# A finer passage into an MLP, z statistics on ScalarE, and eleven GpSimd operations behind VectorE's

## The chip, the cores and the metric

The kernel runs on one core of one Trainium2 chip. The metric is device time in microseconds (us) of one execution, lower is better. A core has TensorE (PE in the profile; PEld is its weight load), VectorE (DVE), ScalarE (ACT), GpSimd (POOL) and SyncE (SP, which here issues DMAs). Each engine runs its own instructions in order and waits on semaphores for the others.

## The reference

One sequence of 2048 rows with 640 channels goes through an adaptive-norm block: a gated long-convolution (an SSM with a short convolution in front), then a gMLP mixer.

```python
mod = (silu(c) @ w_mod)                    # sa, ca, ga, sb, cb, gb, each of 640
h = layernorm(x) * (1 + ca) + sa
x = x + ga * A(h, k, v, ...)               # A: 4-tap shift of k, times v, FFT convolution over 2048, times q
h = layernorm(x) * (1 + cb) + sb
x = x + gb * B(h, ...)

def B(x):
    z = gelu(x @ w_in)                     # 640 -> 1728
    z1 = z[..., :864]
    z2 = layernorm(z[..., 864:])           # mean and variance over 864, per row
    g = w_sp @ z2 + b_sp                   # 2048 x 2048 over the rows
    return (z1 * g) @ w_out                # 864 -> 640
```

## The kernel before, in words

**Parts.** The first part (the convolution) works in five units of 128 channels. It computes the long convolution with matrix products: stage 1, a forward transform per frequency pair (`fwd`), a product with the kernel's transform on VectorE (`prod`, L495), sums `W` of its parts on GpSimd or VectorE (`csum`, L509), an inverse transform (`inv`), and a copy of its result into `Z` on ScalarE (`zc`, L616 calling L278). A last product with the table `Ebd` gives the rows of y.

**The passage.** For units 0 to 3 `Z` is turned by a DMA. For unit 4, the last, TensorE turns it (`zfl`, L831, `last_stage_pe`): four tiles of eight 128x128 flips, two in PSUM slots `pu` and two in `pz`, each copied out whole (`zk`, 1024 elements a partition, two on VectorE and two on ScalarE). Then 32 products of 16 columns (`yl`) for each of four groups of four row tiles; those of the first group come in four pieces of eight. VectorE multiplies with the gate (`yml`, L856), adds the residual (`res`, L808), and takes the statistics of the rows (`ln2`, L814; `ag2`, L943). GpSimd makes 1/sqrt(var + eps) in two operations (`rstd2`, L218 and L219), VectorE -mean*rstd (`nmr2`, L947), and one of three engines normalizes a row tile into `xn2` (`zx`: ScalarE L957, GpSimd L959, VectorE L961). For the first group, in two pieces of two row tiles, TensorE flips the normalized tiles (`hfl`, L972), and VectorE and ScalarE modulate them into `hT` (`hmod`, L985 and L983). The other three groups are turned by a DMA (`turn`) and modulated in place (`hmod2`, L1011 and L1009).

**The z groups.** Sixteen row tiles in four groups. A product of a row tile with half of one half of `w_in` is five matmuls of 432 columns (`zz`, called through the helper L275). There are 64 such products, into the four PSUM slots `pu` and `pz` (two each). ScalarE applies GELU out of PSUM (`gelu`, L1034). The z2 half goes to an `X1` tile, z1 into the memory of the tables `M2` and `G2`. For z2, VectorE takes the statistics of each 432-column piece (`stz`, L1040) and joins them (`agz`, L1044); GpSimd makes the rstd (`rstdz`), VectorE `nmrz` (L1049), and VectorE or ScalarE normalizes (`zn`, L1057, L1055).

**The mixer and the projection.** A two-level Winograd-like scheme over blocks of `w_sp` and z2: sums `S` (L1101) and `T` (L1111), seven products per pair of row tiles (`prodw`, L1126), their joins, DMA turns of u (`turnu`, L1173), the output products (`pp`, `pq`, L1348 and L1335) and the output DMAs.

**What sets the order.** Nothing is scheduled by the compiler. Each operation is recorded with the keys that it reads and writes, and a string `ORDER` of engine letter and operation number sets on which engine and in which place each is emitted (`Plan.run`). Waits follow from the tiles that an instruction touches. `FILLS` is a list of dummy products of `ident` with 512 columns (`fill`) that write a slot nobody reads.

Of the kernel before, what the change touches and what calls it, by code (L numbers as in the profile page):

```python
# [1462 lines left out]
```

## Time and profile before

| | us |
|---|---|
| median of the timed runs (3) | 306.06 (305.61 to 306.27) |
| the profiled execution: its span, first to last instruction | 303.8 |
| between that span and the median | 2.26 |
| TensorE busy in the span | 293.1 |
| VectorE busy | 260.4 |
| GpSimd busy | 186.8 |
| ScalarE busy | 164.0 |

The profiled execution's own time is known by its span. Timeline rows give the start of an instruction in us from the start of the span, its duration, the engine, the line in the kernel, what it writes and reads, and in brackets how long the engine had stood idle and who released it. PEclk is the share of the full clock that TensorE was granted.

### The profile page before, as it was taken

The page shows a single profiled execution, that of the slowest core. Times are in us where ns is not written, and L with a number is a line of the kernel's source. Part 1 is how long each engine was busy: PE and PEld are TensorE (multiplying, and loading weights), DVE is VectorE, ACT ScalarE, POOL GpSimd, SP SyncE. Part 2 cuts the span into 40 slices and gives each one's busy share as a digit, 9 for nine tenths or more (in the row PEclk, how much of TensorE's full clock was granted, in tenths as well). Part 3 has the DMA queues.
Part 4 walks back from the last instruction along what each step waited for, and adds up shares of the span by engine and source line. Part 5 has one row for each costly group of instructions (what it writes and reads, how often), then busy time and mean ns, then how long its engine had stood idle before and what let it go on. Part 6 is the DMA issues. An engine that isn't in the chain of part 4 may idle for free.

```text
span 303.8 us, 7152 instructions
## 1 busy us (share of the span) xinstructions
PE 293.1 (96%) x2827; PEld 207.0 (68%) x2827; DVE 260.4 (86%) x527; ACT 164.0 (54%) x299; POOL 186.8 (61%) x213
## 2 busy tenths in 40 slices
PE   6899999999999999799999999999999999999996
PEld 2788999999989988645555555555555555665664
DVE  8899999999989999989595988988678798886794
ACT  5989999998888865446665779500111102111110
POOL 5463788839769997577537342099531863476771
PEclk9999999999999999869999999999999999999999
DMA  7999869792397978005997900057654446452433
GB/s 143 270 242 271 194 177 282 134 223 39 77 186 163 287 122 276 2 2 105 157 234 154 197 0 4 0 117 150 132 133 90 102 112 141 102 84 73 91 83 121
DMA packets 117155, 41.57 MB, mean 137 GB/s; under 512 B 102557, under 2 KB 117122, under 8 KB 117122
## 3 DMA queue, kind: packets, MB, share of 16 engines
q1 hardware_dynamic: 116968, 41.08, 62.0%
q8 instruction: 22, 0.36, 0.5%
q14 instruction: 11, 0.09, 0.1%
q10 hardware_dynamic: 154, 0.05, 0.1%
HBM read 16.60 MB, written 2.63 MB: 63 GB/s over the span
## 4 chain that ended last, share of the span: by engine, by line
PE 80%; DVE 8%; SPq 5%; DMA 3%; issue 2%; POOL 1%; ACT 0%; DVEq 0%; POOLq 0%
PE ps L1126 23%; PE pu L275 19%; PE pz L275 17%; PE po L1335 5%; PE sm L275 5%; PE s L275 4%; SPq L570 3%; DVE Tf L495 3%; PE po L1348 3%; DMA ZT<-in_A_v_dram 3%; PE pz L1126 2%; PE pu L1126 1%; DVE Z L616 1%; SPq L585 1%; DVE ot L1394 1%
## 5 line engine op out<-in xcount | busy, mean ns | idle before, releaser
L275 PEld LDWEIGHTS <-Z 128*128 128x128 bf16 x320 | 32.0, 100 | 28.8 <-issue 3.0
L275 PE MATMUL pu<-X,M 128*128 128x128 bf16 (+1 forms) x480 | 45.6, 237 | 0.9 <-DVE Tf L495 0.7
L509 POOL TENSOR_TENSOR W<-Tf 128x256 bf16<-128x256 f32 x42 | 30.7, 745 | 15.0 <-DVE Tf L495 9.0
L275 PEld LDWEIGHTS <-M 128*128 128x128 bf16 x480 | 36.7, 98 | 4.2 <-issue 1.6
L1126 PEld LDWEIGHTS <-S 128*128 128x128 bf16 x256 | 25.0, 98 | 20.8
L275 PE MATMUL pu<-big,Z 128*128 128x432 bf16 x160 | 34.6, 360 | 0.0
L278 ACT CAST X<-s 128x1024 bf16<-128x1024 f32 x32 | 32.7, 1021 | 3.3 <-PE s L275 3.2
L275 PE MATMUL pz<-big,Z 128*128 128x432 bf16 x160 | 33.0, 349 | 0.0
L495 DVE TENSOR_TENSOR Tf<-pu,KH 128x1024 f32<-128x1024 f32 x25 | 30.3, 1215 | 1.2 <-ACT Z L278 0.5
L1132 ACT COPY m<-ps 128x432 f32<-128x432 f32 x7 | 3.6, 521 | 49.8 <-PE ps L1126 41.0
L1126 PEld LDWEIGHTS <-wT 128*128 128x128 bf16 x192 | 18.8, 98 | 15.3
L278 ACT CAST Z<-pz 128x512 bf16<-128x512 f32 x40 | 23.5, 596 | 4.9 <-PE pz L275 4.7
L275 PEld LDWEIGHTS <-G 128*128 128x128 bf16 x330 | 24.6, 98 | 1.8 <-issue 0.4
L278 ACT CAST KH<-pu 128x512 bf16<-128x512 f32 x40 | 23.1, 592 | 3.8 <-PE pu L275 3.4
L1126 PE MATMUL ps<-X,wT 128*128 128x432 bf16 x112 | 22.7, 346 | 0.0
L1126 PE MATMUL ps<-X,S 128*128 128x432 bf16 x112 | 22.6, 346 | 0.0
L1040 DVE BATCH_NORM_STATS2 stz<-X 128x6 f32<-128x432 bf16 x32 | 18.1, 588 | 5.0 <-ACT X L1034 4.9
L1126 PE MATMUL ps<-T,S 128*128 128x432 bf16 x112 | 22.2, 346 | 0.0
L275 PE MATMUL sm<-dg,big 128*128 128x128 bf16 x320 | 20.7, 219 | 1.1 <-DVE Z L616 1.0
L275 PEld LDWEIGHTS <-big 128*128 128x128 bf16 x320 | 18.9, 98 | 2.0 <-issue 1.6
L495 DVE TENSOR_TENSOR T<-pu,KH 128x1024 bf16<-128x1024 f32 x15 | 18.2, 1215 | 1.9 <-PE pu L275 1.8
L275 PEld LDWEIGHTS <-X 128*128 128x128 bf16 x288 | 17.8, 98 | 2.2 <-POOL X L433 0.7
(223 smaller groups left out, 666.7 us busy)
## 6 DMA issues: line engine op xcount, KB each, us to landing
wm<-in_w_mod_dram SPq DMA_DIRECT2D x6, 800.0 KB, 4.9
xt<-in_A_q_dram SPq DMA_DIRECT2D x4, 640.0 KB, 5.6
out_dram<-ot SPq DMA_DIRECT2D x15, 160.0 KB, 1.9
big<-in_B_w_in_dram SPq DMA_DIRECT2D x2, 1080.0 KB, 7.8
X<-in_A_ssm_k_dram SPq DMA_DIRECT2D x4, 512.0 KB, 6.2
ZT<-in_A_v_dram SPq DMA_DIRECT2D x1, 1024.0 KB, 7.6
big<-in_A_v_dram SPq DMA_DIRECT2D x1, 1024.0 KB, 7.8
w_o<-in_B_w_out_dram SPq DMA_DIRECT2D x6, 160.0 KB, 3.5
```

Source lines behind the costliest of these rows:

```text
L275: nc.tensor.matmul(o, lhsT=w, rhs=x, start=start, stop=stop)
L278: (e.copy if e is nc.scalar else e.tensor_copy)(dst, src)
L495: e.tensor_tensor(T_[:], (tl[pu] if src is None else tl[src])[:, :, :, None, :].to_broadcast(shape), tl[KH][:, :, None, :, :].to_broadcast ...
L509: e.tensor_tensor(tl[W][:, :, o, :], T_[:, :, 0, o, :], T_[:, :, 1, 1 - o, :], op=ALU.add if o else ALU.subtract)
L570: e.dma_start_transpose(k_of(u)[:, KPAD + h * m:KPAD + (h + 1) * m], A_k[0, h * m:(h + 1) * m, u * DU:(u + 1) * DU])
L585: e.dma_start(v_of(0, ns.start, NT // n) if u0 == 0 else tl[name][:], v_nat[:, ns, ds])
L616: e.tensor_tensor(dst, tl[ps][:].rearrange("p n (c g) -> p n c g", g=8), v_of(u, i * SCH, SCH).rearrange("p n (c g) -> p n c g", g=8), op= ...
L1040: op("D", "stz", lambda e, i=i, n=n, fc=fc: e.bn_stats(out=stz[:, n, fc, :], in_=tl[z2][:, i, fc * FC:(fc + 1) * FC]), r=[(z2, (i, fc))], ...
L1126: nc.tensor.matmul(ps[:, :FC], lhsT=lhs[:, s_, :], rhs=rhs(s_), start=(s_ == 0 and not more), stop=(s_ == HT - 1), skip_group_check=more)
L1132: e.copy(part[p, m][:], part[p, BANK[m]][:, :FC])
L1335: nc.tensor.matmul(ps[:, :HS], lhsT=w(k), rhs=x(k), start=start and k == 0, stop=stop and k == n - 1, skip_group_check=True)
L1348: e.matmul(po[t, i][:, :hi - lo], lhsT=uTs[t][:fsz[ft], ft, :], rhs=T["w_o"][:fsz[ft], ft, lo:hi], start=(ft == 0), stop=(ft == NFT - 1))
```

## The change

Up to the middle of the last unit of the convolution both programs are the same, instruction by instruction. From there on the list `ORDER` is new, and six edits stand behind it:

- The last copy into `Z` (`zc` of step 4 of unit 4) is cut in two.
- The flips of unit 4 and their copies come in halves of four (`zfl`, `zk`, 512 elements), and the first group's `yl` in eight pieces of four.
- For the first two row tiles (`quick`) VectorE adds eps to the variance right after its statistics, so GpSimd makes the rstd in one operation (`rstdq`); `nmr2` is left out, and both tiles are normalized on VectorE. `hfl` flips tile by tile.
- `FILLS` has six more dummy products, in pieces of one, and the list puts them elsewhere.
- For z groups 0 and 1 ScalarE makes the statistics: the GELU of z2 also writes the sum of its outputs (`accum_out`), a new `zsq` squares the row tile with a sum, into memory that z1 of the last row tile takes later, and four small VectorE operations per group (`momz`) turn the sums into mean and variance. `stz` and `agz` of these groups are gone.
- A letter H in the list marks a GpSimd operation that waits until the last VectorE operation ahead of it in the list, of the kinds in `PORT`, has ended. Eleven are marked: `res`, `zx`, `gbm`, two `hmod2`, two `lsm`, `vsum`, two `usum`, `ssum`.

In the rows below `st` and `mv` are the row statistics, `gh` the gated branch, `xt` the residual rows, `s` and `sm` the PSUM slots of the flips, `Z` also the slot of `xn2` and `hT`; X is the z2 tile, M and G hold z1, and stz is where the sums go. The number of an engine's semaphore stands behind its name in a wait.

TensorE at the flips of unit 4, before, each kind of row once:

```order
L831 LDWEIGHTS Z [waits Activation_49]
L831 MATMUL pu<-ident,Z 128x128
L275 LDWEIGHTS ZT
L275 MATMUL sm<-Ebd,ZT 128x64 [waits DVE_49]
L275 MATMUL sm<-Ebd,ZT 128x64
L831 LDWEIGHTS Z
L831 MATMUL pz<-ident,Z 128x128
L831 MATMUL pz<-ident,Z 128x128 [waits PE_49]
```

and now:

```order
L856 LDWEIGHTS Z [waits Activation_49]
L856 MATMUL pu<-ident,Z 128x128
L856 LDWEIGHTS Z
L856 MATMUL pu<-ident,Z 128x128 [waits Activation_49]
L856 MATMUL pz<-ident,Z 128x128
L856 MATMUL pz<-ident,Z 128x128 [waits PE_49]
L856 MATMUL pz<-ident,Z 128x128 [waits DVE_49]
L295 LDWEIGHTS X
L295 MATMUL sm<-Ebd,X 128x4x4 [waits PE_49]
```

The second half of a slot's flips now has a wait of its own on the engine that copies the first half; three of the four slots show one.

VectorE from the statistics of the first two row tiles to their modulation, before:

```order
L814 BN_STATS st_72<-xt 128x6 x2
L943 BN_AGGR mv_82<-st_72 128x2 x2
L856 TENSOR_TENSOR gh<-gh,sm 128x2x128
L808 TENSOR_TENSOR xt<-xt,gh 128x4x128
L808 TENSOR_TENSOR xt<-xt,gh 128x2x128
L947 SCALAR_TENSOR_TENSOR nmr_84<-mv_82,rstd_83 128x2
L814 BN_STATS st_72<-xt 128x6 x4
L943 BN_AGGR mv_82<-st_72 128x2
L856 TENSOR_TENSOR gh<-gh,pz 128x4x128
L985 TENSOR_SCALAR Z<-s_2939,cb_col,sb_col 128x256 x3
```

and now:

```order
L837 BN_STATS st_72<-xt 128x6 x2
L973 BN_AGGR mv_82<-st_72 128x2 x2
L975 TENSOR_SCALAR mv_82<-mv_82 128x2
L884 TENSOR_TENSOR gh<-gh,sm 128x2x128
L884 TENSOR_TENSOR gh<-gh,pz 128x4x128
L831 TENSOR_TENSOR xt<-xt,gh 128x2x128
L993 TENSOR_SCALAR Z<-xt,mv_82,rstd_83 128x640 x2
L837 BN_STATS st_72<-xt 128x6 x2
L1021 TENSOR_SCALAR Z<-s_2920,cb_col,sb_col 128x256 x3
```

`nmr` is gone from the first piece, a small operation on `mv` and two normalizations have come in, and two multiplications with `gh` stand ahead of them. GpSimd there, before and now:

```order
L753 TENSOR_TENSOR gh<-gh,gsa_bf 128x4x128 x2
L218 TENSOR_SCALAR rstd_83<-mv_82 128x2
L219 TENSOR_TENSOR rstd_83<-rstd_83,mhalf 128x2
L959 TENSOR_SCALAR Z<-xt,rstd_83,nmr_84 128x640
L808 TENSOR_TENSOR xt<-xt,gh 128x4x128 x2
L218 TENSOR_SCALAR rstd_83<-mv_82 128x2
L219 TENSOR_TENSOR rstd_83<-rstd_83,mhalf 128x2
```

```order
L831 TENSOR_TENSOR xt<-xt,gh 128x4x128 x3
L238 TENSOR_TENSOR rstd_83<-mv_82,mhalf 128x2
L831 TENSOR_TENSOR xt<-xt,gh 128x4x128
L776 TENSOR_TENSOR gh<-gh,gsa_bf 128x4x128
L236 TENSOR_SCALAR rstd_83<-mv_82 128x2
L238 TENSOR_TENSOR rstd_83<-rstd_83,mhalf 128x2
L991 TENSOR_SCALAR Z<-xt,rstd_83,nmr_84 128x640
```

Of the first rstd's two GpSimd operations one is left, and it normalizes a tile less there.

ScalarE from the first modulation on, before:

```order
L957 ACTIVATE Z<-xt,nmr_84,rstd_83 128x640
L983 ACTIVATE Z<-sm,sb_col,cb_col 128x256 x2
L1034 ACTIVATE X_2980<-pu 128x432
L957 ACTIVATE Z<-xt,nmr_84,rstd_83 128x640
L1034 ACTIVATE M_80<-pz 128x432 x2
L1034 ACTIVATE M_80<-pu 128x432
L983 ACTIVATE Z<-sm,sb_col,cb_col 128x256 x2
L1034 ACTIVATE M_80<-pu 128x432
L957 ACTIVATE Z<-xt,nmr_84,rstd_83 128x640
L1034 ACTIVATE X_2980<-pz 128x432
```

and now:

```order
L1019 ACTIVATE Z<-sm,sb_col,cb_col 128x256 x2
L1071 ACTIVATE X_2983,stz<-pz 128x432
L1071 ACTIVATE X_2983,stz<-pu 128x432
L989 ACTIVATE Z<-xt,nmr_84,rstd_83 128x640
L1071 ACTIVATE X_2983,stz<-pu 128x432
L1019 ACTIVATE Z<-sm,sb_col,cb_col 128x256
L1071 ACTIVATE M_80<-pu 128x432
L1071 ACTIVATE X_2983,stz<-pz 128x432
L1019 ACTIVATE Z<-sm,sb_col,cb_col 128x256
L1071 ACTIVATE M_80<-pz 128x432
L989 ACTIVATE Z<-xt,nmr_84,rstd_83 128x640
```

The rows with `stz` write sums beside their result, and rows of 128x864 that write G are the squares.

The diff, cut to its core (of the list a few lines):

```diff
-FILLS = (4, 2, 2, 2, )
+LAST = 4
+PORT = {"nmr1", "nmr2", "nmrz", "ln1f", "momz", "e2a", "ghm", "res", "csum", "ssum", "xn", "zx", "hmod2", "oa", "usum", "zn", "tsum", "c22b", "lsm", "ox",
+        "c22m", "turns", "vsum", "vsum5", "gbm", "msgn", "mneg", "gneg", "f1m", "e2m", "addD"}
+ACT_STATS = (0, 1)
+FILLS = ((4,), (2,), (2,), (2,), (1, 1, 1), (1, 1, 1))
...
+P737 P739 P731 D740 G677 P727 P741 D732 P743 P746 P748 D698 D699 A738 P745 P747 A728 P744 P742 D749 D750 D751 P1046
+P1047 P1048 D752 P757 D780 P1040 S589 D781 P590 D753 D758 D754 P771 G782 D783 D784 H702 D756 A591 P597 A598 D701 P785
...
-    def run(self, engines):
-        order = [(x[0], int(x[1:])) for x in ORDER.split()]
-        assert sorted(i for _, i in order) == list(range(len(self.ops)))
+    def run(self, engines, tc):
+        nc = tc.nc
+        held = None
+        order = [(x[0].replace("H", "G"), int(x[1:]), x[0] == "H") for x in ORDER.split()]
+        assert sorted(i for _, i, _ in order) == list(range(len(self.ops)))
         done = set()
-        for e, i in order:
+        for e, i, gated in order:
             o = self.ops[i]
             assert e in o["eng"] and done.issuperset(o["deps"]), (e, i)
             if self.late is not None and i >= self.late[0]:
                 self.late[1]()
                 self.late = None
+            made = []
+            if e in "DG":
+                nc.push_inst_callback(made.append)
             o["fn"](engines[e])
+            if e in "DG":
+                nc.pop_inst_callback()
+            if e == "D" and o["kind"] in PORT:
+                held = made[-1]
+            elif gated and held is not None:
+                tc.add_manual_dep(made[0], held.name, mybir.DependencyInfo(mybir.DependencyClass.Sync, mybir.DependencyReason.SCHED_ONLY), reason="port")
             done.add(i)
...
-    def rstd_from_var(dst, var_ap):
-        nc.gpsimd.tensor_scalar(dst, var_ap, EPS, 1.0, op0=ALU.add, op1=ALU.mult)
-        nc.gpsimd.tensor_tensor(dst, dst, mhalf[:, 0:dst.shape[1]], op=ALU.pow)
+    def rstd_from_var(dst, var_ap, eps=True):
+        if eps:
+            nc.gpsimd.tensor_scalar(dst, var_ap, EPS, 1.0, op0=ALU.add, op1=ALU.mult)
+            var_ap = dst
+        nc.gpsimd.tensor_tensor(dst, var_ap, mhalf[:, 0:dst.shape[1]], op=ALU.pow)
...
+            parts = KP if u == NU - 1 and st == LAST else 1
+            for h in range(parts):
+                k0, k1 = h * KP // parts, (h + 1) * KP // parts
+                op("AD", "zc", lambda e, k0=k0, k1=k1: copy(e, tl[Z][:, :, 2 * (KP * st + k0):2 * (KP * st + k1), :], tl[pz][:, k0:k1]
+                                                            .rearrange("p k r (q c) -> p q (k r) c", c=4)),
+                   r=[pz, (Z, "new")], w=[(Z, (st, h) if parts > 1 else st)], n=parts)
...
-            op("GD" if u < NU - 1 else "D", "res", lambda e: e.tensor_tensor(sl, sl, gl, op=ALU.add),
+            op("GD" if u < NU - 1 or g else "D", "res", lambda e: e.tensor_tensor(sl, sl, gl, op=ALU.add),
...
+                for h in range(2):
+                    def flips(e, qb=qb, pt=pt, tag=tag, h=h):
+                        if h == 0:
+                            new(pt, tag, [P, QB, P])
+                        for i in range(h * QB // 2, (h + 1) * QB // 2):
+                            e.transpose(tl[pt][:, i, :], tl[Z][:, qb + i, :, :].rearrange("p j c -> p (j c)"), ident[:])
+
+                    def keep(e, pt=pt, ZT=ZT, low=low, h=h):
+                        if low and h == 0:
+                            new(ZT, "X", [P, 2 * QB, P])
+                        o = h * QB // 2
+                        copy(e, tl[ZT][:, (0 if low else QB) + o:(0 if low else QB) + o + QB // 2, :], tl[pt][:, o:o + QB // 2])
+                    op("P", "zfl", flips, r=["ident"] + [Z] + ([(pt, "new")] if h else []), w=[(pt, h)] + ([] if h else [(pt, "new")]),
+                       new=[] if h else [(pt, tag)], n=4)
+                    fresh = low and h == 0
+                    op("AD", "zk", keep, r=[(pt, h)] + ([] if fresh else [(ZT, "new")]), w=[(ZT, b % 2 * 2 + h)] + ([(ZT, "new")] if fresh else []),
+                       new=[(ZT, "X")] if fresh else [], n=4)
...
-                tag, k = "pz" if g % 2 else "sm", 4 if g == 0 else 1
+                tag, k = "pz" if g % 2 else "sm", 8 if g == 0 else 1
...
+            quick, gs = g == 0 and p == 0, slice(ns[0], ns[-1] + 1)
             for n in ns:
-                op("D", "ag2", lambda e, n=n: e.bn_aggr(out=mv2[:, n, :], in_=st2[:, n, :, :]),
-                   r=[("st2", (u, n)) for u in (1, 3, 4)], w=[("mv2", n)])
-            gs = slice(ns[0], ns[-1] + 1)
-            op("G", "rstd2", lambda e: rstd_from_var(rstd2[:, gs], mv2[:, gs, 1]), r=[("mv2", n) for n in ns], w=[("rs2", (g, p))], n=len(ns))
-            op("D", "nmr2", lambda e: e.scalar_tensor_tensor(nmr2[:, gs], mv2[:, gs, 0], -1.0, rstd2[:, gs], op0=ALU.mult, op1=ALU.mult),
-               w=[("nm2", (g, p))], r=[("rs2", (g, p))])
+                def aggregate(e, n=n):
+                    e.bn_aggr(out=mv2[:, n, :], in_=st2[:, n, :, :])
+                    if quick and n == ns[-1]:
+                        e.tensor_scalar(mv2[:, gs, 1], mv2[:, gs, 1], EPS, None, op0=ALU.add)
+                op("D", "ag2", aggregate, r=[("st2", (u, n)) for u in (1, 3, 4)] + ([("mv2", m) for m in ns[:-1]] if quick and n == ns[-1] else []), w=[("mv2", n)])
+            op("G", "rstdq" if quick else "rstd2", lambda e: rstd_from_var(rstd2[:, gs], mv2[:, gs, 1], not quick), r=[("mv2", n) for n in ns], w=[("rs2", (g, p))], n=len(ns))
+            if not quick:
+                op("D", "nmr2", lambda e: e.scalar_tensor_tensor(nmr2[:, gs], mv2[:, gs, 0], -1.0, rstd2[:, gs], op0=ALU.mult, op1=ALU.mult),
+                   w=[("nm2", (g, p))], r=[("rs2", (g, p))])
...
+                op("D" if quick else "DAG", "zx", norm, r=[("mv2", n), ("rs2", (g, p))] + ([] if quick else [("nm2", (g, p))]) + [("xt", (u, n)) for u in range(NU)] + ([] if first else [(xn2, "new")]),
...
+            halves = ((range(0, 3), "s1"), (range(3, ND), "sm"))
+            for i in range(k):
+                def flips(e, i=i):
+                    for dts, tag in halves:
+                        pt = "ft%d_%d" % (p, dts[0])
+                        if i == 0:
+                            new(pt, tag, [P, len(dts), k, P])
+                        for j, dt in enumerate(dts):
+                            e.transpose(tl[pt][:, j, i, :], tl[xn2][:, i0 + i, dt * P:(dt + 1) * P], ident[:])
+                pts = [("ft%d_%d" % (p, dts[0]), tag) for dts, tag in halves]
+                op("P", "hfl", flips, r=["ident", (xn2, i0 + i)] + [(pt, "new") for pt, _ in pts] * (i > 0),
+                   w=[(pt, i) for pt, _ in pts] + [(pt, "new") for pt, _ in pts] * (i == 0), new=[] if i else pts, n=ND)
...
-                            e.activation(dst, tl[ps][:, :FC], ACT.Gelu_apprx_tanh)
+                            acc = dict(accum_out=zsum[:, n, fc:fc + 1]) if half and g in ACT_STATS else {}
+                            e.activation(dst, tl[ps][:, :FC], ACT.Gelu_apprx_tanh, **acc)
...
+                    if half and g in ACT_STATS:
+                        op("A", "zsq", lambda e, i=i, n=n: e.activation(z1[NT - 1], tl[z2][:, i, :], ACT.Square, accum_out=zsum[:, n, NFC:NFC + 1]),
+                           r=[(z2, (i, fc)) for fc in range(NFC)], w=[("zs", (n, NFC))] + [("z1", (NT - 1, fc)) for fc in range(NFC)])
+                    elif half:
                         op("D", "agz", lambda e, n=n: e.bn_aggr(out=mvz[:, n, :], in_=stz[:, n, :, :]),
                            r=[("stz", (n, fc)) for fc in range(NFC)], w=[("mvz", n)])
+            if g in ACT_STATS:
+                def moments(e, b=slice(ns[0], ns[-1] + 1)):
+                    m, v, t = mvz[:, b, 0], mvz[:, b, 1], zsum[:, b, 0]
+                    e.tensor_tensor(t, t, zsum[:, b, 1], op=ALU.add)
+                    e.tensor_scalar(m, t, 1.0 / Fh, None, op0=ALU.mult)
+                    e.scalar_tensor_tensor(v, t, 1.0 / Fh, m, op0=ALU.mult, op1=ALU.mult)
+                    e.scalar_tensor_tensor(v, zsum[:, b, NFC], 1.0 / Fh, v, op0=ALU.mult, op1=ALU.subtract)
+                op("D", "momz", moments, r=[("zs", (n, i)) for n in ns for i in range(NFC + 1)], w=[("mvz", n) for n in ns])
```

More of the change, by code (lines that the diff above doesn't have):

```diff
@@ L108 @@
[L108 to L111 removed]
+G5 D18 A1 S83 G0 G110 S2 P7 S23 G109 G6 D13 A4 D14 G25 A16 D15 D111 P1039 D10 S26 D112 P8 A38 D17 D113 A11 G89 D130
@@ L231 @@
     mvz = persist.tile([P, NT, ADIM], F32)
+    zsum = stz[:, :, 0, 0:NFC + 1]
     rstdz = persist.tile([P, NT], F32)
@@ L823, in last_stage_pe @@
                 pt, ZT, low = "pt%d_%d" % (u, qb), "ZT%d_%d" % (u, b // 2), b % 2 == 0
-                ZTs.append((ZT, b % 2))
+                ZTs += [(ZT, b % 2 * 2 + h) for h in range(2)]
                 tag = "pz" if b % 2 else "pu"
-                def flips(e, qb=qb, pt=pt, tag=tag):
-                    p_ = new(pt, tag, [P, QB, P])
-                    for i in range(QB):
-                        e.transpose(p_[:, i, :], tl[Z][:, qb + i, :, :].rearrange("p j c -> p (j c)"), ident[:])
@@ L961, in norm @@
                         e.tensor_scalar(dst, xt[:, n, :], mv2[:, n, 0:1], rstd2[:, n:n + 1], op0=ALU.subtract, op1=ALU.mult)
-                op("DAG", "zx", norm, r=[("mv2", n), ("rs2", (g, p)), ("nm2", (g, p))] + [("xt", (u, n)) for u in range(NU)] + ([] if first else [(xn2, "new")]),
+                op("D" if quick else "DAG", "zx", norm, r=[("mv2", n), ("rs2", (g, p))] + ([] if quick else [("nm2", (g, p))]) + [("xt", (u, n)) for u in range(NU)] + ([] if first else [(xn2, "new")]),
                    w=[(xn2, n % TB)] + ([(xn2, "new")] if first else []), new=[(xn2, "Z")] if first else [])
@@ L966, in flip_piece @@
             k, i0 = len(ns), ns[0] % TB
-            for dts, tag in ((range(0, 3), "s1"), (range(3, ND), "sm")):
-                def flips(e, dts=dts, tag=tag):
-                    p_ = new("ft%d_%d" % (p, dts[0]), tag, [P, len(dts), k, P])
-                    for j, dt in enumerate(dts):
-                        for i in range(k):
-                            e.transpose(p_[:, j, i, :], tl[xn2][:, i0 + i, dt * P:(dt + 1) * P], ident[:])
-                pt = "ft%d_%d" % (p, dts[0])
-                op("P", "hfl", flips, r=["ident"] + [(xn2, i0 + i) for i in range(k)], w=[pt], new=[(pt, tag)], n=len(dts) * k)
+            halves = ((range(0, 3), "s1"), (range(3, ND), "sm"))
[10 more added lines that the diff above has]
+                   w=[(pt, i) for pt, _ in pts] + [(pt, "new") for pt, _ in pts] * (i == 0), new=[] if i else pts, n=ND)
             for dt in range(ND):
@@ L1175 @@
         early = [i for i, o in enumerate(plan.ops) if o["kind"] not in
-                 ("ag2", "rstd2", "nmr2", "zx", "hfl", "hmod", "turn", "hmod2", "zz", "gelu", "stz", "agz", "rstdz", "nmrz", "zn", "fill",
+                 ("ag2", "rstd2", "rstdq", "nmr2", "zx", "hfl", "hmod", "turn", "hmod2", "zz", "gelu", "zsq", "momz", "stz", "agz", "rstdz", "nmrz", "zn", "fill",
                   "ldwi", "ln2")]
```

161 lines of the change are left out of this document (76 added, 85 removed).

## The prediction

> **What bounds the kernel now.** I read the page first, then the windows by stage, then the waits of TensorE, then the timeline where it waits.
>
> ```profile
> PE   6899999999999999799999999999999999999996
> PEclk9999999999999999869999999999999999999999
> ```
>
> TensorE is full in almost every slice, and its clock is full but for the two slices from 121.5 to 136.7 us. Windows of 10 and 20 us say it in numbers (length, then busy us of each engine, then the granted clock):
>
> ```profile
> 100.00:120.00 20.00, 18.76 (x302) 17.51 (x300) 19.00 (x27) 14.17 (x25) 18.41 (x22) 1.00 0.83 230
> 120.00:130.00 10.00, 7.79 (x195) 6.58 (x193) 9.38 (x29) 4.29 (x7) 5.36 (x7) 0.85 0.10 35
> 140.00:150.00 10.00, 10.00 (x57) 5.37 (x55) 8.77 (x29) 5.80 (x13) 7.40 (x8) 1.00 0.98 150
> 160.00:170.00 10.00, 10.00 (x57) 5.34 (x56) 6.28 (x14) 5.70 (x12) 6.93 (x8) 1.00 0.78 158
> ```
>
> From 140 us on TensorE never stops, so work taken from VectorE there (8.77 of 10) buys nothing by itself. What can be won lies between 119 and 134 us, the passage, where TensorE stands still for more than 2 us and then runs at half speed. TensorE's two longest waits of the passage:
>
> ```profile
> PE s L972 <- POOL Z L959: 1.4, 1, 1.4
> PE s L275 <- DVE Z L985: 0.8, 1, 0.8
> ```
>
> The chain behind them, from the last copy into `Z` to the first `zz`:
>
> ```profile
> 117.72 1.30 ACT L278 CAST Z<-pz 128x512 bf16<-128x512 f32 x2 [0.53 <-PE pz L275]
> 119.08 1.07 PE L831 MATMUL pu<-ident,Z 128*128 128x128 bf16 x16 [0.44 <-ACT Z L278]
> 119.74 0.69 DVE L278 COPY X<-pu 128x1024 bf16<-128x1024 bf16 x1 [0.17 <-PE pu L831]
> 120.21 1.06 PE L831 MATMUL pz<-ident,Z 128*128 128x128 bf16 x16
> 121.31 1.01 ACT L278 COPY X<-pz 128x1024 bf16<-128x1024 bf16 x1
> 122.81 0.40 DVE L856 TENSOR_TENSOR gh<-gh,sm 128x256 bf16<-128x256 bf16 x1
> 122.82 1.76 PE L275 MATMUL pz<-Ebd,X 128*128 128x16 bf16 x64
> 124.43 0.19 POOL L218 TENSOR_SCALAR rstd<-mv 128x2 f32<-128x2 f32 x1 [3.34 <-DVE mv L943]
> 124.70 0.81 POOL L219 TENSOR_TENSOR rstd<-rstd,mhalf 128x2 f32<-128x2 f32 x1
> 125.55 0.16 DVE L947 SCALAR_TENSOR_TENSOR nmr<-mv,rstd 128x2 f32<-128x2 f32 x1 [0.41 <-POOL rstd L219]
> 126.81 0.67 PE L972 MATMUL s<-ident,Z 128*128 128x128 bf16 x6 [1.43 <-POOL Z L959]
> 127.91 0.72 DVE L985 TENSOR_SCALAR Z<-s,cb_col,sb_col 128x256 bf16<-128x256 bf16 x2
> 128.69 1.03 PE L275 MATMUL s<-ident 128*128 128x512 bf16 x2 [0.78 <-DVE Z L985]
> 129.51 3.81 PE L275 MATMUL pu<-big,Z 128*128 128x432 bf16 x10
> 133.11 2.35 PE L275 MATMUL pz<-big,Z 128*128 128x432 bf16 x10
> ```
>
> And the clock (third number from the right) in stretches of 2 us:
>
> ```profile
> 124.00:126.00 2.00, 1.38 (x55) 1.28 (x52) 1.59 (x9) 0.25 (x1) 1.13 (x3) 1.00 0.04 8
> 126.00:128.00 2.00, 1.10 (x10) 0.84 (x10) 1.96 (x7) 0.67 (x2) 2.00 (x3) 0.75 0.00 0
> 128.00:130.00 2.00, 1.31 (x4) 0.56 (x5) 2.00 (x6) 1.02 (x2) 1.14 (x2) 0.50 0.00 0
> 132.00:134.00 2.00, 2.00 (x7) 0.86 (x6) 2.00 (x7) 0.91 (x2) 1.94 (x2) 0.54 0.00 0
> ```
>
> 0.75 over 126 to 128 puts the halving at 127.0, and 0.54 over 132 to 134 puts its end at 133.84: 6.83 us, of which the `zz` products lie in the last 4.33. A product of five matmuls takes 0.91 us later:
>
> ```profile
> 147.72 1.08 PE L275 MATMUL pu<-big,Z 128*128 128x432 bf16 x5
> 148.63 1.08 PE L275 MATMUL pz<-big,Z 128*128 128x432 bf16 x5
> ```
>
> 148.63 - 147.72 = 0.91, 0.18 a matmul; the ten at 129.51 take 133.11 - 129.51 = 3.60, 0.36 each.
>
> **The change part by part.** Up to the middle of the last unit nothing differs, so all terms start at the last `zc`.
>
> *Halves of zc and of the flips.* The last `zc` in two halves ends about where it ended (117.72 + 1.30 = 119.02; each half pays its fixed part again, +0.05 to +0.1). Its forerunner on GpSimd and the queue ahead are the same. The flips gain less than their halving suggests: a slot's second four flips wait for the copy of the first four, so the halves of a slot follow each other. A slot takes four halves in turn (two tiles of eight). For each: four flips 1.07/4 = 0.27, some 0.15 until the copy starts (119.74 against the eighth flip at 119.62), and the copy of 512, half of 0.69 or of 1.01 plus a fixed part, which I put at 0.42 on VectorE and 0.58 on ScalarE. 4 x 0.42 + 2 x (0.42 + 0.58) = 3.7, from 119.1 to 122.8, then two pieces of `yl`, 0.4: 123.2 to 123.4. Before it was 122.8, where the multiplication at 122.81 starts. So +0.5 on this stretch; bounds -0.3 (the copies overlap as the halving means) and +0.7 (every half pays ScalarE's price).
>
> *The rstd and the two normalizations.* Before, from that multiplication to `pow`, 124.70 - 122.81 = 1.89. The eps operation on GpSimd goes, with its hand-over 124.70 - 124.43 = 0.27, and comes back on VectorE at about the 0.16 of `nmr`: -0.1. `pow` stays, 125.55 - 124.70 = 0.85 with its hand-over. Then before: `nmr` and the slower of ScalarE's and GpSimd's row tile, 126.81 - 125.55 = 1.26. Now two on VectorE, which the trace has later:
>
> ```profile
> 137.40 0.79 DVE L961 TENSOR_SCALAR Z<-xt,mv,rstd 128x640 bf16<-128x640 bf16 x2
> 137.53 1.32 POOL L959 TENSOR_SCALAR Z<-xt,rstd,nmr 128x640 bf16<-128x640 bf16 x1 [1.64 <-ACT Z L983]
> ```
>
> 0.79 plus some 0.1 for what VectorE has under way: -0.35. With 0.5 - 0.1 - 0.35 the first `hfl` stands at about 126.9, where it stood (126.81). The chain to the flips is therefore not shorter; what one edit takes the others give.
>
> *From the flips to the first zz.* Before, the ten flips and the modulations end at 127.91 + 0.72 = 128.63, then the two dummy products, which the list puts behind the wait for `hmod`, hold TensorE from 128.69 to 129.51: 0.82 us on the path, at half clock. In the new list no dummy product stands between `hfl` and `zz` (the last two stand ahead of a later group's `yl`), and the first `zz` needs its five parts of `hT` one after another, so it can start before the last modulation ends. First `zz` at 128.5 to 128.8; I take 128.5: -1.0. Bounds -0.7 (it waits for the last one) and -1.1.
>
> *The clock.* If TensorE keeps its clock the 4.33 us from 129.51 to 133.84 shrink to half: -2.16. That hangs on how much TensorE does. I count the columns it streams, at 0.91 us for 2160 of them. In the 3.4 us up to 127.0 there are some 64 products of 16 columns and at most three flips, 1400 columns, 0.6 us, 17%: after that the clock fell. In the 3.4 us before, 120.2 to 123.6, there are 16 flips of 128 and some 70 products of 16, 3200 columns, 39%: the clock stayed. The new list puts five dummy products of 512 into the gap, three behind the first group's `yl` and two behind the second's, and spreads the other groups' `yl` between them: with the ten flips 2560 + 1536 + 1280 + 150 = 5500 columns in the 5.4 us from 123.1 to 128.5, 43%, and in its worst 3.4 us about 33%. That is nearer to 39 than to 17, so I take the clock as kept; bounds 0 and -2.16.
>
> *z statistics on ScalarE.* Off VectorE go 16 `stz`, half of these 18.1 us, and eight `agz`; `momz` and four normalizations come back. VectorE gains a few us and TensorE nothing. The cover is ScalarE's idle time, and it must suffice:
>
> ```profile
> 22.45 0.74 ACT L666 ACTIVATE gh<-xt 128x640 bf16<-128x640 bf16 x1
> 23.09 0.18 ACT L666 ACTIVATION_READ_ACCUMULATOR gh<-xt 128x1 f32 x1
> 23.18 0.56 ACT L278 CAST KH<-pu 128x512 bf16<-128x512 f32 x1
> 142.87 0.95 ACT L1034 ACTIVATE X<-pu 128x432 bf16<-128x432 f32 x2
> L1040 DVE BATCH_NORM_STATS2 stz<-X 128x6 f32<-128x432 bf16 x32 | 18.1, 588 | 5.0 <-ACT X L1034 4.9
> L1034 ACT ACTIVATE X<-pu 128x432 bf16<-128x432 f32 x16 | 8.4, 532 | 8.7 <-PE pu L275 8.7
> L1055 ACT ACTIVATE X<-X,nmrz,rstdz 128x864 bf16<-128x864 bf16 x8 | 8.8, 1104 | 0.0
> ```
>
> A sum is read out by an instruction of its own, 0.18 us, which overlaps: the next starts 0.09 later (23.18 - 23.09). Two GELUs in a row take 0.95, so one occupies 0.95 - 0.53 = 0.42. A row tile now asks ScalarE for two plain GELUs 0.84, two with sums 1.02, a square of 864 (0.64 x 864/640 = 0.86) with a sum 0.95: 2.81 us, against TensorE's 4 x 0.91 = 3.64. Over eight row tiles 22.5 of 29.1, and some 5 us of normalizations and modulations beside them: 95% full. Hidden, without much to spare: price 0. If nothing overlapped, a tile would take 2 x 0.53 + 2 x 0.71 + 1.10 + 0.18 = 3.76, with the 5 us 35.1: +6.0. The row at 23.18 is the same engine with the same read-out, so I go by the low end.
>
> *The eleven held operations.* A held operation, and all of GpSimd behind it, waits for one VectorE operation, 0.2 to 1.2 us. What is late next are `xn2` of group 1 and the sums `u`, then their turns on SP's queue. The mixer's turns have room:
>
> ```profile
> 206.01 2.56 SPq L1173 DMA_TRANSPOSE uT<-u  x2
> 212.51 2.07 PE L1348 MATMUL po<-w_o,uT 128*128 128x320 bf16 x14
> ```
>
> 208.57 to 212.51 is 3.9 us, more than three holds. On the other side a normalization on GpSimd took 1.32 beside VectorE's (row at 137.53), so waiting may shorten what waits. Neither is on TensorE's path: 0, bounds -0.2 and +0.6 (one hold of 1.2 that reaches a `zz`, half of it covered).
>
> The sum: -1.0 - 2.16 - 0.0 = -3.2. The span goes from 303.8 to 300.6. The median of the runs is 2.26 above the span (306.06), so the time is 302.9.
>
> **The rivals.**
>
> *The clock falls all the same.* [...] Then the dummy products are no loss, and the half-speed stretch moves with its start. Begun at 124 to 126 it ends one to three us earlier than 133.84 and costs about half that less; begun at 127 or later it costs what it cost. With the -1.0 at the first `zz`, worth half at half speed, it is -0.5 to -1.7: 304.4 to 305.6, say 305.2.
>
> [...]
>
> *ScalarE becomes the bound.* This is the slower side. The place is z groups 0 and 1, 128 to 160 us. The point from which it decides: 24 instructions with sums have 29.1 - 27.5 = 1.6 us to spare, 0.07 each; beyond that TensorE waits for `pu` or `pz`, and at 0.07 + 3.2/24 = 0.20 each more than I count, the whole gain is gone. At the high end above (0.32 more each) the time is 302.9 + 6.0 = 308.9; with half of it lost to overlap elsewhere about 307. Against it: the row at 23.18. For it: GELUs here read PSUM, and ScalarE takes the first two `zx` and `hmod` in the same stretch.
>
> *The passage does not shorten.* The halves cost +0.7, the held `res` and `zx` delay group 1, the first `zz` waits for the last `hmod`, and the clock falls: about 306.0, no change.
>
> **How the numbers follow.** The clock kept: 0.58, 302.9, its own range 302.2 to 303.8 from the bounds of the small terms. The clock lost: 0.22, 305.2. ScalarE bound: 0.11, 307 to 309. No shortening: 0.09, 306.0. The range goes from 302.1 to 306.0 and leaves out the third case and half of the fourth. Differences within 0.2% (0.6 us) can't be told from none. Faster by more: the first case and four fifths of the second, 0.76; the same: the rest of the second and most of the fourth, 0.12; slower: the third and a little of the fourth, 0.12.
>
> **What would show it.** The granted clock 1.00 in every 2 us from 120 to 140, and ten `zz` matmuls in 1.8 us instead of 3.60, carry two thirds of the forecast; the first `zz` at 128.5 with no row of `s<-ident` ahead of it after the flips carries the rest; the first `hfl` still near 126.9 would confirm that the edits ahead of it cancel. READ_ACCUMULATOR rows followed by the next GELU within 0.1 us, and no wait of TensorE for L1071 from 130 to 165, show the statistics hidden. A wait of `pu` or `pz` on ScalarE there, or a clock of 0.50 beyond 124, would make it wrong.

## The result and the profile after

The changed kernel takes 303.30 us (median of 4 runs, 302.62 to 303.54) against 306.16 us of the kernel before (4 runs, 305.61 to 306.63) on the same chip: a ratio of 0.9912, 95% interval 0.9889 to 0.9934. The profiled execution has a span of 301.8 us and took 303.54.

The page's first lines, and windows of 10 and 2 us (columns as in the prediction: length, busy us of PE, PEld, DVE, ACT, POOL, granted clock, DMA share, GB/s):

```profile
PE   6898999999999999899999999999999999999996
PEclk9999999999999999999999999999999999999999
```

```profile
120.00:130.00 10.00, 9.07 (x216) 7.48 (x212) 8.81 (x27) 4.11 (x10) 5.64 (x7) 1.00 0.25 92
...
124.00:126.00 2.00, 1.87 (x47) 1.38 (x45) 1.59 (x6) 0.48 (x1) 0.00 (x0) 1.00 0.00 0
126.00:128.00 2.00, 2.00 (x69) 1.76 (x65) 1.97 (x9) 0.17 (x1) 0.71 (x1) 1.00 0.04 8
128.00:130.00 2.00, 2.00 (x50) 1.68 (x46) 2.00 (x8) 1.25 (x3) 1.52 (x2) 1.00 0.00 0
```

The clock stays at 1.00 throughout, and between 120 and 130 us TensorE is busy 9.07 us instead of 7.79. TensorE's waits above 0.5 us that are left, by the view of waits:

```profile
PE sm L295 <- POOL ident L340: 2.6, 1, 2.6
PE sm L295 <- DVE Z L639: 1.8, 2, 1.1
PE pu L856 <- ACT X L298: 0.7, 1, 0.7
PE pu L295 <- DVE Tf L515: 0.7, 2, 0.5
```

The two waits of the passage for normalization (1.4) and modulation (0.8) are gone; a new one of 0.7 stands at the flips of unit 4 (L856), which wait for a copy on ScalarE. The passage in the timeline:

```profile
119.81 0.65 ACT L298 CAST Z<-pz 128x256 bf16<-128x256 f32 x2 [0.70 <-PE pz L295]
120.51 0.40 PE L856 MATMUL pu<-ident,Z 128*128 128x128 bf16 x4
121.00 0.58 ACT L298 COPY X<-pu 128x512 bf16<-128x512 bf16 x1 [0.54 <-PE pu L856]
121.63 0.61 PE L856 MATMUL pu<-ident,Z 128*128 128x128 bf16 x8 [0.73 <-ACT X L298]
124.83 0.42 DVE L884 TENSOR_TENSOR gh<-gh,sm 128x256 bf16<-128x256 bf16 x1 [0.34 <-PE sm L295]
126.65 0.71 POOL L238 TENSOR_TENSOR rstd<-mv,mhalf 128x2 f32<-128x2 f32 x1 [2.89 <-DVE mv L975]
127.41 0.28 DVE L831 TENSOR_TENSOR xt<-xt,gh 128x256 bf16<-128x256 bf16 x1
127.61 0.80 DVE L993 TENSOR_SCALAR Z<-xt,mv,rstd 128x640 bf16<-128x640 bf16 x2
128.17 0.57 PEld L1007 LDWEIGHTS <-Z 128*128 128x128 bf16 x10
129.56 1.12 PE L295 MATMUL pz<-big,Z 128*128 128x432 bf16 x5
130.51 1.81 PE L295 MATMUL pu<-big,Z 128*128 128x432 bf16 x9
```

All of it stands later than forecast, and the reason lies 95 us ahead of the change. VectorE's wait there for the transfer of v, in the kernel before and then in the changed one:

```profile
24.40 1.29 DVE L616 TENSOR_TENSOR Z<-sm,ZT 128x512 bf16<-128x512 f32 x2 [0.51 <-DMA ZT<-in_A_v_dram]
```

```profile
25.64 1.29 DVE L639 TENSOR_TENSOR Z<-sm,ZT 128x512 bf16<-128x512 f32 x2 [1.45 <-DMA ZT<-in_A_v_dram]
```

The instructions are the same up to there, so these 1.24 us belong to the execution and not to the change: in the profiles of the experiments below, most of them the changed kernel with an edit behind this place, the first flips, 119.08 and 120.51 in these two, start anywhere from 118.83 to 120.36. The difference of the spans, stretch by stretch:

| stretch | before | after | difference | forecast |
|---|---|---|---|---|
| start to first flips (of it 1.24 the transfer) | 119.08 | 120.51 | +1.43 | 0.0 |
| flips to the multiplication | 3.73 | 4.32 | +0.59 | +0.5 |
| multiplication to `pow` | 1.89 | 1.82 | -0.07 | -0.1 |
| `pow` to the first `hfl` | 2.11 | 1.52 | -0.59 | -0.35 |
| first `hfl` to the first `zz` | 2.70 | 1.39 | -1.31 | -1.1 |
| first `zz` to the end | 174.29 | 172.24 | -2.05 | -2.16 |
| sum | 303.8 | 301.8 | -2.00 | -3.2 |

Without the 1.24 us the sum is -3.24.

### The profile page after: what moved, and what is told of

Its sections match the earlier page's. It is cut to its first block, busy times and chain, and to the rows that moved or that the text cites. A ratio compares the mean times of both kernels' runs of the same rounds, so it can differ in the third digit from the quotient of the medians.

```text
span 301.8 us, 7181 instructions
## 1 busy us (share of the span) xinstructions
PE 292.3 (97%) x2833; PEld 207.2 (69%) x2833; DVE 255.2 (85%) x527; ACT 168.2 (56%) x329; POOL 174.4 (58%) x203
## 4 chain that ended last, share of the span: by engine, by line
PE 83%; DVE 6%; SPq 6%; DMA 3%; issue 1%; ACT 1%; DVEq 0%; ACTq 0%
PE ps L1177 23%; PE pu L295 19%; PE pz L295 18%; PE sm L295 6%; PE po L1386 6%; PE s L295 4%; SPq L593 3%; PE po L1399 3%; DMA ZT<-in_A_v_dram 3%; DVE Tf L515 2%; PE pz L1177 2%; PE pu L1177 1%; DVE Z L639 1%; SPq L608 1%; DVE ot L1445 1%
## 5 line engine op out<-in xcount | busy, mean ns | idle before, releaser
L295 PEld LDWEIGHTS <-Z 128*128 128x128 bf16 x320 | 31.2, 98 | 26.8 <-DVE Z L1021 0.2
L295 PE MATMUL pu<-big,Z 128*128 128x432 bf16 x160 | 32.6, 346 | 0.0
L298 ACT CAST Z<-pz 128x512 bf16<-128x512 f32 (+1 forms) x41 | 23.4, 586 | 5.1 <-PE pz L295 5.0
L1185 ACT ACTIVATE m<-ps,bcol 128x432 f32<-128x432 f32 x7 | 4.3, 621 | 29.5 <-PE ps L1177 29.5
```

The costliest lines, as they stand in the source:

```text
L295: nc.tensor.matmul(o, lhsT=w, rhs=x, start=start, stop=stop)
L298: (e.copy if e is nc.scalar else e.tensor_copy)(dst, src)
L1185: e.activation(part[p, m][:], part[p, BANK[m]][:, :FC], ACT.Identity, bias=T["bcol"][:, p + HT:p + HT + 1], scale=1.0)
```

## The experiments

Each was timed beside the kernel before, on one chip per group. The ratio is to the runs of before in the same group, with its 95% interval. The last column counts runs by their mean granted clock. A halving over the 6.83 us of the profile before takes 3.4 of 303.8 us away, which is 0.989; half as long a halving gives 0.994, and one and a half times as long 0.983.

Up to the first flips of unit 4 the changed kernel and its variants run the same instructions, and in their profiles that takes from 119.03 to 120.51 us. So differences of 1 us are best read from there to the end of the span: 303.8 - 119.08 = 184.7 us before, 301.8 - 120.51 = 181.3 in the changed kernel, and 181.2 in a second profile of it (301.6 - 120.36).

| kernel | median us | ratio | runs by clock |
|---|---|---|---|
| before (29 runs in one group) | 305.74 | 1 | 20 at 0.989, 9 at 0.983 |
| changed | 302.97 | 0.9910 (0.9887 to 0.9932) | 6 of 6 at 1.00 |
| before with gap products | 303.22 | 0.9918 (0.9897 to 0.9939) | 5 at 1.00, 1 at 0.994 |
| before without path products | 303.97 | 0.9946 (0.9928 to 0.9965) | 6 at 0.994, 6 at 0.989 |
| changed without gap products | 303.79 | 0.9938 (0.9915 to 0.9960) | 4 at 0.994, 2 at 0.989 |
| changed, three gap products | 304.08 | 0.9945 (0.9923 to 0.9968) | 1 at 1.00, 7 at 0.994, 4 at 0.989 |
| changed, statistics on VectorE | 308.02 | 1.0078 (1.0052 to 1.0104) | 4 at 1.00, 2 at 0.994 |
| changed without holds | 306.20 | 1.0017 (0.9999 to 1.0036) | 7 at 0.994, 5 at 0.989 |
| changed, one hold | 302.10 | 0.9896 (0.9877 to 0.9916) | 5 of 5 at 1.00 |
| changed, flips slot by slot | 301.41 | 0.9853 (0.9830 to 0.9877) | 4 of 4 at 1.00 |
| the last two together | 301.41 | 0.9858 (0.9839 to 0.9877) | 4 of 4 at 1.00 |

### Do the dummy products alone carry the gain?

The edit to the kernel before, with no other part of the change:

```diff
-FILLS = (4, 2, 2, 2, )
+FILLS = (4, 2, 2, 2, 3, 2)
...
             def fill(e, i=i, k=k):
+                if i == 1:
+                    return
```

In its list the three stand behind the first group's last `yl`, the two behind the second group's; product 1, which is left out, is the pair between the modulation and the first `zz`.

> The kernel before with one thing of the change alone: five dummy products in the gap (three behind the first group's yl, two behind the second's) and the two between the modulation and the first zz left out. The rest of the passage, the list and the statistics are those of before. If the clock and the two products on the path carry the gain, as the prediction has it (-2.16 and -0.8), the granted clock stays 1.00 and the time is 303.1 to 303.5, as good as the whole change. If the shorter chain of the passage carries it, the clock may stay but the time is above 304.5. If the dummy products don't hold the clock without the finer passage, the time is 305.3 or more.

Measured: 303.22 us, ratio 0.9918. The changed kernel, timed against the same kernel before, has 0.9910, and the intervals overlap almost wholly: by these times nothing is left for the finer passage, the new list, the statistics and the holds together. The traces are finer. From the first flips to the end this kernel takes 301.3 - 118.83 = 182.4 us, 2.3 less than before, and the changed kernel 181.3, 1.2 less again; ahead of the flips the changed kernel spends some 0.2 of that (+1.43 in the table above, of it 1.24 the transfer). So the dummy products carry 2.3 of some 3.3 us, and the rest brings about 1, which the scatter of the times hides. Its `hfl` and the first `zz`:

```profile
118.83 1.07 PE L833 MATMUL pu<-ident,Z 128*128 128x128 bf16 x16 [0.44 <-ACT Z L280]
...
126.56 0.51 PE L974 MATMUL s<-ident,Z 128*128 128x128 bf16 x6 [0.34 <-POOL Z L961]
127.70 2.27 PE L277 MATMUL pu<-big,Z 128*128 128x432 bf16 x10 [0.41 <-DVE Z L987]
129.81 1.99 PE L277 MATMUL pz<-big,Z 128*128 128x432 bf16 x10
132.75 0.51 PE L974 MATMUL s<-ident,Z 128*128 128x128 bf16 x6 [0.95 <-POOL Z L961]
```

From the first flips to the first `zz` it takes 8.87 us, less than the changed kernel's 9.05. It then loses 0.95 us at the second piece of the first group, where the changed kernel has no wait; that is most of the 1.2.

The other half of that experiment takes the pair off the path and puts nothing into the gap:

```diff
-                if i == 1:
+                if i in (1, 4, 5):
                     return
```

> The kernel before without the two dummy products between the modulation and the first zz, and nothing put into the gap. If those two lie on the path as the prediction has it (0.82 us at half clock), the first zz starts up to 0.8 us earlier, but at half speed half of that is lost again: 0.3 to 0.5 us less than before. Rival: without them TensorE streams less in that stretch and the clock comes back later: no gain, or up to 1 us more.

Measured: 303.97 us, by the ratio 1.65 us less, over three times what was expected. The pair is on the path, as expected. But there is more, and some of it lies in the clock: by their mean clock half of the runs now have one stretch of half speed (0.994) and half two (0.989), where before has two or three (0.989 and 0.983). The runs with two have a median of 304.19 us, against 305.38 for the runs of before with two; the rest comes from the stretch that the other runs are spared. So the pair cost twice, by its own time (0.82 us) and by a longer half speed in half of the runs. Why the half speed is shorter without the pair no run shows.

### Does the finer passage hold the clock without them?

```diff
                 def fill(e, i=i, h=h, k=k):
+                    if i in (1, 5):
+                        return
```

> The changed kernel without the five dummy products in the gap; nothing else differs. Theory: the stretch up to the first flips of the first row tiles falls to some 17 to 25% of full streaming, the clock halves for 6.83 us, and the time is 304.5 to 305.6 (the rival of the prediction, 305.2). Rival: the finer passage keeps TensorE busy enough by itself, the clock stays 1.00 and the time is 303.2 to 303.5.

Measured: 303.79 us, and no run of six kept the clock. Its windows of 0.2 us, and TensorE's rows in that time:

```profile
126.40:126.60 0.20, 0.00 (x0) 0.00 (x0) 0.20 (x2) 0.00 (x0) 0.00 (x0) 0.50 0.00 0
...
129.60:129.80 0.20, 0.20 (x2) 0.12 (x1) 0.20 (x2) 0.00 (x0) 0.08 (x1) 0.50 0.00 0
129.80:130.00 0.20, 0.20 (x3) 0.10 (x2) 0.20 (x2) 0.00 (x0) 0.12 (x2) 0.97 0.00 0
```

```profile
126.71 0.50 PE L1007 MATMUL s<-ident,Z 128*128 128x128 bf16 x3 [0.94 <-DVE Z L993]
...
127.75 1.05 PE L295 MATMUL sm<-Ebd,X 128*128 128x16 bf16 x32
128.65 1.63 PE L295 MATMUL pz<-big,Z 128*128 128x432 bf16 x5
```

Half speed from 126.4 to 129.8, 3.4 us, half of the 6.83 of before; two runs had it twice as long (0.989). The theory holds for the fall of the clock. The price was put too high: 304.5 to 305.6 was expected for two stretches, and the two runs with two took 304.48 and 304.68, the low end, while four runs had only one and took 303.15 to 303.85. In the profile the single stretch lies mostly on waits, flips and `yl` (until 128.65) and not on `zz`.

With three products kept (the condition is `i == 1`):

> The changed kernel with three of the five dummy products, those behind the first group's yl. The gap then has 1024 columns less, 4500 instead of 5500 in 5.4 us, 35%, and in its worst 3.4 us some 25%. If the clock hangs on how full a stretch of 3.4 us is, with a bound between 17 and 33%, the runs differ: some keep the clock (303.3) and some lose it for one such stretch (mean clock 0.994, 0.3 to 1.2 us more). Rival: three are as good as five, every run at 1.00.

Measured: one run of twelve kept the clock (302.38 us), seven lost it once, four twice. Three are far nearer to none than to five. The same program gives 0, 1 or 2 stretches from run to run, as the expectation supposes; what decides between them no run shows. In the profile of three products the clock falls at 128.57:

```profile
128.00:130.00 2.00, 2.00 (x31) 1.23 (x28) 2.00 (x9) 0.96 (x2) 1.89 (x3) 0.64 0.00 0
```

In the 3.41 us ahead of that, half of the 6.83, TensorE streamed 25 single columns, 64 products of 16, eleven of 128 and the first part of a `zz`, some 2640 columns. At 2160 in 0.91 us, 3.41 us have room for 8100, so this is 33%.

### The statistics

The groups whose statistics ScalarE makes are set to none (`ACT_STATS = ()`), and in the list each `stz` stands behind its GELU, `agz` behind these.

> The changed kernel with the statistics of z groups 0 and 1 back on VectorE (16 bn_stats and 8 bn_aggr, each behind its GELU in the list; no squares, no sums on ScalarE). Theory of the prediction: TensorE is the bound there and VectorE's relief buys it nothing: within 0.5 us of the changed kernel, 303.0 to 303.8. Rival: the new list has given VectorE work that was GpSimd's, and with 9.4 us of statistics more it delivers the turned row tiles of groups 2 and 3 late: TensorE waits in the z stage, 305 to 308.

Measured: 308.02 us, 1.7% above the changed kernel. The rival holds. The wait that costs TensorE most (3.7 us in four times), and two windows:

```profile
PE pu L296 <- DVE Z L1048: 3.7, 4, 1.4
```

```profile
140.00:150.00 10.00, 8.69 (x47) 4.29 (x46) 9.86 (x32) 4.64 (x9) 1.05 (x2) 1.00 0.39 82
160.00:170.00 10.00, 7.48 (x40) 3.55 (x38) 9.86 (x26) 4.73 (x10) 3.25 (x4) 1.00 0.94 158
```

L1048 is `hmod2`, the modulation of the turned tiles of groups 1 to 3. VectorE is busy 9.86 of 10 us and brings it late. One window of the kernel before and one of the changed kernel say why:

```profile
130.00:170.00 40.00, 40.00 (x218) 21.20 (x217) 31.55 (x97) 23.63 (x47) 25.01 (x28) 0.95 0.70 137
```

```profile
130.00:170.00 40.00, 40.00 (x228) 21.77 (x228) 34.30 (x106) 33.05 (x82) 17.70 (x21) 1.00 0.69 125
```

Though half of its z statistics are gone, VectorE works 34.30 us there instead of 31.55; GpSimd has lost 7.3 us and ScalarE gained 9.4. The list has handed VectorE GpSimd's work: in that stretch 8 of the residual additions of 512 columns run on VectorE instead of 3, and 9 of the normalizations instead of 6. With this list the statistics had to leave to make room. The place of the 24 operations in the list was not tuned, so the 5 us are a price of this list, not of the statistics as such.

### The holds

Every H in the list becomes a G:

```diff
-... D784 H702 D756 ...
+... D784 G702 D756 ...
```

> The changed kernel with the eleven GpSimd operations free to start as soon as their data are there. The prediction puts the holds at 0 (bounds -0.2 and +0.6): TensorE has no wait from 130 us on, with or without them, so the time is within 0.3 us of the changed kernel. Rival: VectorE's operations beside GpSimd's get longer, turned tiles come late and TensorE waits in the z stage: 0.5 to 1.5 us more.

Measured: 306.20 us, no better than the kernel before. The loss is far above the bounds, and at another place than the rival had it. The timeline of VectorE and GpSimd ahead of the first `hfl`, and the window of 2 us that follows:

```profile
126.74 1.15 POOL L831 TENSOR_TENSOR xt<-xt,gh 128x512 bf16<-128x512 bf16 x1
126.81 1.23 DVE L831 TENSOR_TENSOR xt<-xt,gh 128x256 bf16<-128x256 bf16 x1
127.85 1.20 POOL L776 TENSOR_TENSOR gh<-gh,gsa_bf 128x512 bf16<-128x512 bf16 x1
127.97 1.62 DVE L993 TENSOR_SCALAR Z<-xt,mv,rstd 128x640 bf16<-128x640 bf16 x2
129.29 0.50 PE L1007 MATMUL s<-ident,Z 128*128 128x128 bf16 x3 [1.64 <-DVE Z L993]
```

```profile
128.00:130.00 2.00, 0.71 (x7) 0.71 (x8) 2.00 (x5) 0.00 (x0) 1.05 (x1) 0.55 0.00 0
```

The same two VectorE rows took 0.28 and 0.80 in the changed kernel. Here each begins about 0.1 us after a GpSimd operation has begun, and the first of each row is done only after that one has ended: the addition at 126.81 + 1.23 = 128.04, GpSimd's at 126.74 + 1.15 = 127.89. The 1.62 is a first normalization of 1.27 and an ordinary second of 0.44, which overlap a little. That is +0.95 and +0.82 on the path to the first flips; TensorE waits 1.64 us, and the clock falls in every run (0.55 over 128 to 130 us in this one, a mean of 0.994 or 0.989 in all twelve).

What makes the two VectorE operations longer no row shows; measured is 1.23 and 1.27 us instead of 0.28 and 0.44, beside GpSimd operations of 1.15 and 1.20.

In the changed kernel the held addition begins at 128.48, after the two normalizations. Only that hold was left in the next run:

> The changed kernel with one of the eleven holds left, that of the residual addition (res) that stands behind the two normalizations of the first piece; the ten others are free. In the run without any hold all of the loss that its trace shows lies at that place: there res and the multiplication behind it ran beside VectorE's addition and its first normalization, which took 1.23 and 1.27 us instead of 0.28 and 0.44. If that is the whole cause, this run is as good as the changed kernel (0.991 of before, clock 1.00 in nearly all runs). If the ten others matter too, TensorE waits for a tile of a later group and it is 0.5 to 1.5 us more.

Measured: 302.10 us, ratio 0.9896, all five runs at 1.00, as good as the changed kernel with all eleven. From the first flips to the end its profile has 300.3 - 119.03 = 181.3 us, the same as the changed kernel's. One hold does it; the ten others show no effect.

### The halves of a slot

The list gives the half flips of all four slots first, then the second halves, and ScalarE and VectorE still copy four each, with two of the halves exchanged between them:

```diff
-... P733 A734 P735 D736 P725 A726 P729 D730 P737 P739 P731 D740 G677 P727 P741 D732 P743 P746 P748 D698 D699 A738 P745 P747 A728 P744 P742 ...
+... P733 P737 P725 P729 A734 D738 A726 D730 P735 P739 P727 P731 A736 D740 G677 P741 P745 P747 P743 A728 D732 P748 P746 P744 P742 D698 D699 ...
```

> The changed kernel with the eight half tiles of flips of unit 4 in another order: the first halves of all four slots, then the second halves, and four of the eight copies on each of VectorE and ScalarE. The prediction says that halves of a slot follow each other because the second waits for the copy of the first, and that this costs 0.5 us. If so, with other slots in between the waits are covered, the last yl of the first group ends about 1.1 us earlier and the time falls by 0.8 to 1.2 us, to 302.1 to 302.5. Rival: the copies set the pace or the first normalization is held by other work of VectorE, and the time stays within 0.3 us of 303.3.

Measured: 301.41 us, ratio 0.9853, below the changed kernel's 0.9910 with intervals that do not meet: faster than both kernels. Its timeline:

```profile
119.30 0.40 PE L856 MATMUL pu<-ident,Z 128*128 128x128 bf16 x4
119.53 0.39 PE L856 MATMUL pz<-ident,Z 128*128 128x128 bf16 x4
...
119.78 2.13 ACT L298 COPY X<-pu 128x512 bf16<-128x512 bf16 x4 [0.55 <-PE pu L856]
...
122.55 0.40 DVE L884 TENSOR_TENSOR gh<-gh,sm 128x256 bf16<-128x256 bf16 x1
...
127.26 1.18 PE L295 MATMUL pz<-big,Z 128*128 128x432 bf16 x5
```

From the flips to the multiplication 3.25 us instead of 4.32, and to the first `zz` 7.96 instead of 9.05: -1.1, as expected. TensorE's wait of 0.7 at the flips is gone. From the first flips to the end it takes 299.5 - 119.30 = 180.2 us, 1.1 less than the changed kernel, so the gain of the passage reaches the end whole. The medians differ by 1.6 between the kernels (301.41 and 302.97). The half microsecond more lies ahead of the first flips, where the programs are the same (119.30 against 120.51 in the profiles), and is not the order's. What was expected of both findings together:

> Both findings together: the half flips of all four slots first, as in the run on their order, and only the hold of res behind the first two normalizations. Each alone gave a ratio to before of 0.985 and 0.990. If the ten other holds are indifferent the ratio is 0.985 again; if one of them costs something, 0.983.

Measured: 0.9858, the same as the order of the flips alone, and again 180.2 us from the first flips to the end (299.6 - 119.37).

## Why the prediction was right, and where not

Forecast 302.9 (302.1 to 306.0), measured 303.30. By its steps:

*The clock, -2.16.* Right: -2.05 in the trace, every run of the changed kernel at 1.00. But the count behind it was off, and here the forecast had luck. That 3.4 us, half of the 6.83, is the stretch to count over was the author's estimate; no run shows over which stretch the clock is decided, only that the half speed lasted 3.4 us in some profiles and 6.8 in others. The prediction put the new list at 33% in its worst 3.4 us; counted in the rows of its timeline, the emptiest 3.41 us of the changed kernel (from 126.55) hold some 3350 columns, 41%. Falls came after 15% (without gap products), 18% (before) and 33% (three products, where the expectation had 25); the 41% of the kernel before from 120.18 to 123.59, put at 39 in the prediction, kept the clock. By this a list that really held 33% might have lost the clock. It might also have kept it: the profile of before with gap products has the clock at 1.00 though its emptiest stretch (from 123.15) holds 32%. So this count alone does not tell the runs that fall from those that don't, and one program gave 0, 1 and 2 stretches of half speed from run to run (three gap products: mean clocks of 1.00, 0.994 and 0.989), which the trace of one execution could not show.

*First zz, -1.0.* Right in size, and the split of the stretch was right too: the chain to `hfl` comes out at +0.59 - 0.07 - 0.59 = -0.07 (forecast 0.0), the rest at -1.31. That the edits ahead of `hfl` cancel is confirmed by the experiment that has none of them: before with gap products takes 126.56 - 118.83 = 7.73 us from the first flips to `hfl`, the changed kernel 128.17 - 120.51 = 7.66.

*Halves of a slot, +0.5.* Right: +0.59, and the order that avoids the wait gains 1.1.

*The statistics, 0.* The cover on ScalarE was rightly priced. A GELU with a sum and the square behind it, in the changed kernel:

```profile
137.65 0.53 ACT L1071 ACTIVATE X<-pu 128x432 bf16<-128x432 f32 x1
138.08 0.19 ACT L1071 ACTIVATION_READ_ACCUMULATOR X<-pu 128x1 f32 x1
138.17 0.92 ACT L1082 ACTIVATE G<-X 128x864 bf16<-128x864 bf16 x1
```

The read-out holds the next operation back by 0.09 (138.17 - 138.08), and TensorE has no wait from 130 to 170. The sentence "VectorE gains a few us and TensorE nothing" holds for the whole execution, where VectorE is busy 255.2 us instead of 260.4, and failed in the stretch that counts: it took VectorE's other work as that of before, and from 130 to 170 us the list had added more than the statistics took away (34.30 against 31.55 us). Without the edit this list is 5 us slower.

*The held operations, 0 with bounds -0.2 and +0.6.* This step failed. It asked what a hold costs and never what VectorE's operations cost without it. The sum used 0.79 for two normalizations on VectorE, a row in which GpSimd began later (137.53 against 137.40) and was the one that took longer (1.32 instead of 0.87). That price is true only because `res` is held; free, it is 1.62, and another 0.95 in front of it. The row at 137.53 showed the lengthening in the other direction, and the prediction read it as a cost to GpSimd alone. The forecast came out right because the change holds the one operation on which it depends.

*The time from the span.* The 2.26 us were partly chance: in the later runs of both kernels the time is about 1.8 above the span of the same execution, so the profiled execution of before was about 0.5 faster than its median. The late transfer at the start worked the other way in the profile after.

The rival of a lost clock (305.2) was overpriced by 1.4 to 2.1 us for one stretch and 0.5 to 0.7 for two (303.15 to 303.85 and 304.48 to 304.68 without gap products); 0.5 of that is the distance from span to time just named.

## What to carry to other kernels

Where TensorE waits in a short passage before a long full stretch, price the clock behind the wait before the wait itself: here five dummy products put into the gap and two taken off the path bring 2.3 of the some 3.3 us that the traces show for the whole rewrite. When a step on the critical path is moved to VectorE, look at what GpSimd starts beside it, and hold that one operation; here the one hold on the path was worth 3 us or more (306.20 us without holds, 302.97 with all, 302.10 with it alone) and the ten others nothing. Cutting work into halves helped here only once the halves of different buffers alternated: +0.59 us without that, 1.1 less with it. Before reading a difference of 1 us off two medians, compare the traces from the first place where the programs differ.

## What the runs showed of the hardware that was not expected

A VectorE addition of 0.28 us took 1.23, and a normalization of 0.44 took 1.27, each time with a GpSimd operation of 1.15 to 1.20 us begun 0.1 us earlier; with GpSimd beginning later, VectorE kept its time and GpSimd's normalization rose from 0.87 to 1.32. In these rows the one that started first kept its time (GpSimd's addition 1.15 as in the changed kernel, VectorE's two normalizations 0.79), and the other took longer.

In the five profiles with a fall of the clock the half speed lasted 3.4 us (changed without gap products, and with three) or 6.8 (before, before without path products, changed without holds), and the mean clocks of all runs stand near 1.00, 0.994, 0.989 and 0.983. Even the kernel before has 0.989 in some runs and 0.983 in others, about 1 us apart: 304.65 to 306.50 us (median 305.38) and 305.88 to 306.67 (median 306.35). Part of what looks like noise in its times is this, and part is the start, which differs by up to 1.5 us ahead of the first flips (119.03 to 120.51 in the profiles of the changed kernel and its variants).
